# Summing the first two gate-and-up products in PSUM, and one form of the down projection for all tokens

## The chip, the cores and the metric

The kernel runs on one core of a Trainium2 chip. The core has five engines that each work through their own queue in program order and meet through semaphores: TensorE (PE in the profile; its weight loads are shown apart as PEld), VectorE (DVE), ScalarE (ACT), GpSimd (POOL) and SyncE (SP), which issues most of the DMAs. Matmuls write to PSUM, eight banks of 2 KB per partition; VectorE and ScalarE read and write PSUM and SBUF.

The metric is the device time of one execution in microseconds, the median of several. Lower is better.

## The reference

The input `x` has 2048 tokens of 448 features. The first half is an FNet mixing layer: with `n = layernorm(x)`, `h = x + Cr (n Hr) - Ci (n Hi)`, where `Cr`, `Ci` are the 2048x2048 cosine and sine matrices over the tokens and `Hr`, `Hi` those over the features. The second half is a gated feed-forward layer:

```
g = layernorm(h) @ w_gate          # 448 -> 1792
u = layernorm(h) @ w_up            # 448 -> 1792
out = h + (gelu(g) * u) @ w_down   # 1792 -> 448
```

All inputs and the output are float32.

## The kernel before

**Precision.** Every float32 operand is split in two float16 numbers, a high part (ScalarE copies the float32 tile to float16, `hi_part`, line 107) and a low part (VectorE subtracts the high part, `lo_part`, lines 111 and 113). One product is then three float16 matmuls: high x high, high x low, low x high.

**Seven products.** Large products are done in Strassen form: a 2x2 block product with seven instead of eight block products, with sums of blocks as operands and sums of results afterwards. `STRASSEN` (line 155) lists the operands for the down projection.

**Stages.** Up to about 346 us the kernel does the mixing layer and prepares the feed-forward weights, which it splits and stores to DRAM. Then comes the feed-forward layer, in 56 steps, `t = 0` to 55. The tokens are in four blocks of 512 (`q = t // 14`); in a block the 14 steps go over the tiles of 128 hidden features (`f`). A step is one `GateUp` object: the Strassen form of a pair of gate and up over one hidden tile, two token halves of 256. It has seven products into three PSUM tiles of 128x256, X, Y and Z, each of five or six matmuls (`product`, matmul at line 1015), 39 in all:

- `open`: X = A11 B11, Y = S2 T2. ScalarE copies X to SBUF as `u1` (line 1053), VectorE makes `u2 = Y + u1` (line 1025).
- `z_open`: Z = S1 T1.
- `xy`: X += A12 B21 and Y += S3 T3. ScalarE makes `g1 = gelu(X)` (line 1066), VectorE makes `u3 = Y + u1` and the hidden value `Z + u3`.
- `yz`: Y += A22 T4 and Z += S4 B22. VectorE makes the other hidden value `Y + u1`, GpSimd multiplies it by `g1` (line 1082).
- `c12_plus`: VectorE makes `c12 = Z + u2`; `c_last`: ScalarE takes its Gelu (line 1089) and GpSimd multiplies it into the first hidden value (line 1091).

From step 14 on, each step also does one unit `d = t - 14` of the down projection: 21 matmuls (`dn_mm`, line 963) on 128 tokens of each of the four quarter tiles `(hidden half, token half)`, summed over seven units into seven half banks `a0` to `a3`. Before that, `dn_sums` (GpSimd lines 1108 and 1109, VectorE line 1110) makes the five operand sums of the unit and `dn_split` its high and low parts. After seven units a `Drain` adds the seven sums to `h` (ScalarE copies two banks, VectorE adds from the banks, GpSimd adds the copies) and the result is stored.

**Other work.** The down weights are loaded, summed and split by `down_prep` in steps 0 to 13. The operands of blocks 2 and 3 are prepared in steps 14 to 40 by entries of the table `side`: an entry `(t, k)` is emitted at the k-th call `do(t, k)` of step t. The entries of `ffn_norm_act` (VectorE line 229, ScalarE line 231) stand at `k = 1` of steps 14, 20, 28 and 34; a drain begins at `k = 2` of steps 20, 27, 34, 41 and 48. At step 5 ScalarE takes a square root for the last layer normalisation and then returns to the Gelu table.

**The last block before.** For `q = 3` the hidden values go to `hq` and are split whole into `last["h"]`; the down weights are loaded a second time and the two missing weight blocks are split into `last["w"]`. After the last step, tokens with `j = 1` of the block are done in the plain form by `last_mm` (line 1178), two passes of 84 matmuls of 128x224. Meanwhile `last_sums` and `last_split` make the Strassen operands of the tokens with `j = 0`, which `last_pair_mm` (line 1220) then does in 147 matmuls, the last three units ordered by product so that their sums can be drained and stored one after the other (line 1434).

**Order.** The schedule is written by hand: each engine does its instructions in the order in which the program emits them. In a main step before, that is

```
cur.z_open(); prev.c_last(); do(t, 0); dn_split(d + 1)
dn_mm(d, range(0, 8)); cur.xy(); dn_ahead(t)
dn_mm(d, range(8, 18)); do(t, 1); do(t, 4)
cur.yz(); cur.c12_plus(); dn_mm(d, range(18, 21))
do(t, 5); do(t, 2); do(t, 3); cur = GateUp(t + 1); cur.open()
```

Of the kernel before, what the change touches and what calls it, by code (L numbers as in the profile page):

```python
# [8 lines left out]
F16 = mybir.dt.float16  # L9
# [23 lines left out]
def kernel(  # L33
# [922 lines left out]
    def strassen_mm(acc, a_of, b_of, first, last, products):  # L956

        for n in products:
            k, m = divmod(n, 3)
            a, b = STRASSEN[k]  # L960
            la, lb = ((0, 0), (0, 1), (1, 0))[m]

            PE.matmul(  # L963
                acc[k // 2][:, k % 2 * HD : (k % 2 + 1) * HD],
                a_of(la, a),
                b_of(lb, b),
                start=first and m == 0 and k % 2 == 0,
                stop=last and m == 2,
                skip_group_check=True,
            )  # L970


# [11 lines left out]
    def down_prep(t):  # L984

        n, odd = divmod(t, 2)
        if odd:
# [6 lines left out]
        elif n < NC:  # L994
            down_hi(n, 0)
            down_lo(n, 0)
            down_hi(n, 1)
# [32 lines left out]
    hh, hq = {}, {}  # L1030

    class GateUp:


        def __init__(self, t):
            self.t, self.name = t, f"{t}"
            self.q, self.f = divmod(t, NF)

            self.own = self.q > 0 or self.f % 2 == 0

        def bank(self, k):
            pool, tag = (ps_gu, "XYZ"[k]) if self.own else (ps_dn, f"a{k}")
            return pool.tile([P, 512], F32, tag=tag, name=f"p{'XYZ'[k]}_{self.name}")[:, :TQ]
# [4 lines left out]
        def open(self):  # L1048
# [4 lines left out]
            A.activation(self.u1, self.X, AF.Copy, scale=SC)  # L1053
            self.u2 = ftile("u2", 2, f"u2_{self.name}")
            plus(self.u2, self.Y, self.u1)

        def z_open(self):
            self.Z = self.bank(2)
            self.mul(self.Z, "S1", "T1", True)

        def xy(self):
            mul = [lambda: self.mul(self.X, "A12", "B21", False), lambda: self.mul(self.Y, "S3", "T3", False)]
            for m in mul if self.q == 0 else mul[::-1]:
                m()
            self.g1 = ftile("g1", 1, f"g1_{self.name}")
            A.activation(self.g1, self.X, AF.Gelu_apprx_tanh, scale=1.0 / (X_SC * W_SC))  # L1066
            u3 = ftile("u3", 1, f"u3_{self.name}")
            plus(u3, self.Y, self.u1)
            plus(self.hidden(1), self.Z, u3)

        def hidden(self, g):
            if self.q == 3:
                return hq[self.t][:, g, :]
            k, n = divmod(self.f, NF // 2)
            return hh[self.q][:, n, 2 * k + g, :]

        def yz(self):
            self.mul(self.Y, "A22", "T4", False)
            self.mul(self.Z, "S4", "B22", False)
            c21 = self.hidden(0)  # L1080
            plus(c21, self.Y, self.u1)
            G.tensor_mul(c21, c21, self.g1)  # L1082

        def c12_plus(self):
            self.c12 = ftile("c12", 1, f"c12_{self.name}")
            plus(self.c12, self.Z, self.u2)
# [6 lines left out]
    def gw_load(t):  # L1093
        gw[t] = w_tile(f"gw{t}")
        nc.sync.dma_start(gw[t], w_dram[t % NF])
# [8 lines left out]

    def dn_sums(d):
        t = dn_hid(d)
        s = dn_s[d] = late.tile([P, 5, P], F32, tag="dn_s", bufs=2, name=f"dn_s{d}")
# [3 lines left out]

    def dn_split(d):
        w = dn_w[d] = late.tile([P, 2, 7, P], F16, tag="dn_w", bufs=3, name=f"dn_w{d}")
        for src, dst in ((dn_hid(d)[:, 0:4:3], slice(0, 2)), (dn_s.pop(d), slice(2, 7))):
            hi_part(w[:, 0, dst], src)
            lo_part(w[:, 1, dst], src, w[:, 0, dst])

    outr = out.rearrange("(k g j p) d -> k j p g d", k=2, g=2, j=4)

    def dn_mm(d, products=range(21)):  # L1120
        p, n = divmod(d, NC)
        if n == 0 and 0 in products:
            acc_d[p] = [ps_dn.tile([P, 512], F32, tag=f"a{k}", name=f"acc_d{p}_{k}") for k in range(4)]
        w = dn_w[d]
        strassen_mm(
            acc_d[p],
            lambda l, a: w[:, l, a, :],
            lambda l, b: wd[n][:, l, b, :],
            n == 0,
            n == NC - 1,  # L1130
            products,
        )
# [13 lines left out]

    last = {}

    def last_begin():
        last["h"] = fpool.tile([P, 2, NF, 2 * TQ], F16, tag="hh", bufs=2, name="h_last")  # L1150
        w = ring.tile([P, N_OPS, 2 * P], F16, tag="ops", bufs=2, name="w_last")
        w = w.rearrange("p o d -> p (o d)")[:, : 4 * NC * HD]
        last["w"] = w.rearrange("p (l n k d) -> p l n k d", l=2, n=NC, k=2)

    def last_hi(t):
        hi_part(last["h"][:, 0, t % NF], hq[t].rearrange("p g t -> p (g t)"))

    def last_lo(t):
        h = last["h"][:, :, t % NF]
        lo_part(h[:, 1], hq.pop(t).rearrange("p g t -> p (g t)"), h[:, 0])  # L1160

    def last_w_hi(n):
# [335 lines left out]
```

## Time and profile before

| | |
|---|---|
| Median of 3 runs | 713.66 us (713.15 to 714.07) |
| Span of the profiled execution | 711.7 us |
| TensorE busy | 706.9 us, 5517 matmuls |
| VectorE busy | 572.3 us |
| ScalarE busy | 323.5 us |
| GpSimd busy | 235.6 us |
| Granted TensorE clock | 1.00 in all stages |

The profiled execution's time is given as its span, from the first to the last instruction; the runs are timed around it. In the profile, "idle before, releaser" is the time an engine stood still before an instruction and what ended that wait. Matmuls overlap their successors, so a group of six shown as 0.82 us takes 0.66 us of TensorE's time; the chain of work shows the latter. Lines such as L1025 or L107 are helpers that many callers share; the names of the tiles tell them apart.

### The profile page before, as it was taken

To read this page: it belongs to the slowest core of one execution; us is meant where nothing else is said; L and a number is where in the kernel's file an instruction comes from. 1 tells how busy PE (TensorE), PEld (TensorE's weight loads), DVE (VectorE), ACT (ScalarE), POOL (GpSimd) and SP (SyncE) were. 2 spreads that over 40 slices of the span, in tenths; PEclk is the share of its full clock that TensorE was granted. 3 is DMA by queue.
4 is the path that set the end of the run, shared out by engine and by line. 5 is a ranking of instruction groups with operands and counts; after the bars stand their busy time and mean duration, and the time that the engine had idled before them with its cause. 6 is when DMAs were issued, how large, how long until landed. Compare 5 with 4: busy or idle time off the path is not lost.

```text
span 711.7 us, 14303 instructions
## 1 busy us (share of the span) xinstructions
PE 706.9 (99%) x5517; PEld 536.4 (75%) x5517; DVE 572.3 (80%) x1194; ACT 323.5 (45%) x612; POOL 235.6 (33%) x277
## 2 busy tenths in 40 slices
PE   9999999999999999999999999999999999999998
PEld 6555555555555555797978899999999999999998
DVE  7997648596958979998767788787787877989787
ACT  5776424263617554543335444442444434354331
POOL 0000000000000000000365866576686766858441
PEclk9999999999999999999999999999999999999999
DMA  8798548999999989553698425648448576555401
GB/s 271 249 251 261 118 179 224 292 321 258 291 331 282 313 285 272 207 142 108 163 381 310 157 79 167 189 162 203 177 136 248 182 209 211 191 215 208 156 28 53
DMA packets 102613, 150.92 MB, mean 212 GB/s; under 512 B 61072, under 2 KB 72464, under 8 KB 102544
## 3 DMA queue, kind: packets, MB, share of 16 engines
q1 hardware_dynamic: 102400, 149.09, 68.0%
q10 hardware_dynamic: 144, 0.92, 0.4%
q8 instruction: 43, 0.70, 0.4%
q14 instruction: 26, 0.21, 0.1%
HBM read 115.90 MB, written 20.19 MB: 191 GB/s over the span
## 4 chain that ended last, share of the span: by engine, by line
PE 99%; DVE 0%; ACT 0%; POOL 0%; issue 0%; ACTq 0%; POOLq 0%
PE acc L626 33%; PE pY L1015 15%; PE acc_d L963 12%; PE pX L1015 9%; PE pZ L1015 9%; PE y L691 9%; PE acc_f L498 7%; PE last_a L1220 2%; PE last_X L1178 1%; PE last_tr L1178 1%; PE pw L101 1%; PE last_Y L1220 0%; DVE e L526 0%; ACT zs L107 0%; DVE hr L1434 0%
## 5 line engine op out<-in xcount | busy, mean ns | idle before, releaser
L626 PE MATMUL acc<-xs,ws 128*128 128x448 f16 x1248 | 237.9, 352 | 0.0
L626 PEld LDWEIGHTS <-ws 128*128 128x128 f16 x1248 | 122.1, 98 | 113.8
L1015 PEld LDWEIGHTS <-gw 128*128 128x128 f16 x1755 | 171.4, 98 | 17.2
L209 POOL TENSOR_TENSOR wd_s<-wd 128x448 f32<-128x448 f32 x7 | 8.0, 1140 | 351.0 <-DVE r_h L141 342.5
L1015 PE MATMUL pY<-hops,gw 128*128 128x256 f16 x765 | 105.3, 273 | 0.0
L963 PE MATMUL acc_d<-wd,dn_w 128*128 128x224 f16 x882 | 105.1, 259 | 0.0
L963 PEld LDWEIGHTS <-dn_w 128*128 128x128 f16 x882 | 85.0, 98 | 2.9
L113 DVE SCALAR_TENSOR_TENSOR ws<-wr,ws 128x1024 f16<-128x1024 f32 (+2 forms) x66 | 75.1, 1140 | 7.0 <-ACT ws L107 5.3
L107 ACT ACTIVATE ws<-wr 128x1024 f16<-128x1024 f32 (+2 forms) x66 | 64.4, 981 | 28.2 <-DMA wr<-in_w_seq_dram 26.7
L1025 DVE SCALAR_TENSOR_TENSOR u<-pY,u 128x256 f32<-128x256 f32 x112 | 47.0, 419 | 30.5 <-ACT c L1089 18.9
L1015 PE MATMUL pX<-hops,gw 128*128 128x256 f16 x495 | 68.7, 273 | 0.0
L1015 PE MATMUL pZ<-hops,gw 128*128 128x256 f16 x495 | 68.4, 273 | 0.0
L691 PE MATMUL y<-wh,z 128*128 128x448 f16 x336 | 66.2, 352 | 0.0
L1066 ACT ACTIVATE g<-pX 128x256 f32<-128x256 f32 x56 | 21.4, 383 | 81.3 <-PE pX L1015 74.2
L1053 ACT ACTIVATE u<-pX 128x256 f32<-128x256 f32 x56 | 21.5, 383 | 80.9 <-PE pX L1015 80.8
L691 PEld LDWEIGHTS <-z 128*128 128x128 f16 x336 | 32.9, 98 | 29.6
L111 DVE TENSOR_TENSOR dn_w<-dn_s,dn_w 128x640 f16<-128x640 f32 x42 | 52.8, 1258 | 1.1 <-ACT dn_w L107 0.8
L1082 POOL TENSOR_TENSOR hh<-hh,g 128x256 f32<-128x256 f32 x42 | 31.1, 739 | 55.8 <-DVE hh L1025 53.3
L498 PEld LDWEIGHTS <-ws 128*128 128x128 f16 x504 | 48.3, 98 | 0.9
L1091 POOL TENSOR_TENSOR hh<-hh,c 128x256 f32<-128x256 f32 x42 | 38.2, 910 | 17.9 <-ACT c L1089 17.9
L1108 POOL TENSOR_TENSOR dn_s<-hh 128x256 f32<-128x256 f32 x42 | 43.6, 1039 | 0.0
L1109 POOL TENSOR_TENSOR dn_s<-hh 128x256 f32<-128x256 f32 x42 | 43.3, 1030 | 0.0
(144 smaller groups left out, 1020.4 us busy)
## 6 DMA issues: line engine op xcount, KB each, us to landing
gw<-w_dram SPq DMA_DIRECT2D x45, 896.0 KB, 5.2
wr<-in_w_seq_dram SPq DMA_DIRECT2D x100, 256.0 KB, 4.9
w_dram<-gu_w SPq DMA_DIRECT2D x14, 896.0 KB, 6.3
gu_raw<-in_w_gu_dram SPq DMA_DIRECT2D x28, 384.0 KB, 5.9
wr<-in_w_seq_dram SPq DMA_DIRECT2D x14, 512.0 KB, 5.5
wd<-in_w_down_dram SPq DMA_DIRECT2D x14, 448.0 KB, 4.0
gw_first<-w_dram SPq DMA_DIRECT2D x7, 896.0 KB, 5.2
x<-in_x_dram SPq DMA_DIRECT2D x16, 224.0 KB, 3.8
```

The source lines that it names most:

```text
L107: A.activation(dst, src, AF.Copy, scale=scale)
L111: V.tensor_sub(dst, src, hi)
L113: V.scalar_tensor_tensor(dst, src, scale, hi, op0=ALU.mult, op1=ALU.subtract)
L498: PE.matmul(fast_sum(n, k), fast_a(n, i, lw, a), fast_b(j, lx, b), start=j == 0 and m == 0 and k % 2 == 0, stop=j == NT // 2 - 1 and m == ...
L626: PE.matmul(acc[key][:, :D], w[:, lw, block * P : (block + 1) * P], xs[c][:, lx, :], start=c == 0 and m == 0, stop=c == NT - 1 and m == 2,)
L691: PE.matmul(y[:, :D], z[p][:, lz, k, g * P : (g + 1) * P], wh[:, lw, k, :], start=k == 0 and m == 0, stop=k == 6 and m == 2,)
L963: PE.matmul(acc[k // 2][:, k % 2 * HD : (k % 2 + 1) * HD], a_of(la, a), b_of(lb, b), start=first and m == 0 and k % 2 == 0, stop=last and ...
L1015: PE.matmul(ps, w[:, wl, wa + ws, :], ops[:, m + ms, :], start=first and n == 0, stop=last and n == len(terms) - 1, skip_group_check=True,)
L1025: V.scalar_tensor_tensor(dst, ps, SC, other, op0=ALU.mult, op1=ALU.add)
L1091: G.tensor_mul(c22, c22, self.c12)
L1108: G.tensor_add(s[:, 0:2], t[:, 0:2], t[:, 2:4])
L1109: G.tensor_sub(s[:, 2:4], t[:, 1:4:2], t[:, 0:4:2])
```

## The change

**Gate and up.** The seven products and their 39 matmuls stay, in the order `x1, y1, x2, z1, y2, z2, y3`. After X = A11 B11 ScalarE copies X into the PSUM tile Y, and S2 T2 is added onto that copy by TensorE (no `u1`). ScalarE reads Y as `u2`, then S3 T3 is added to the same Y; ScalarE reads Z = S1 T1 as `m5`, and VectorE makes the second hidden value from Y and `m5`. Then A22 T4 is added to Y, and VectorE multiplies it by `g1` in one operation (no GpSimd multiplication there). `c12` is Z plus `u2` as before. From block 1 on, Y of odd steps lies in the bank `tr`.

**Order.** In the first block, parts of `down_prep` of the next step stand before `y2` and after the copy. In a main step all side work stands at the end.

**The last block.** Its hidden tiles go to `hh` like the others, in the order f = 0, 7, 1, 8, ... (`f_of`), so units of it are complete during the block. Eight units (`EARLY`) are summed and split in steps 44 to 55 into buffers that are free by then; the other six follow in the tail. All of its tokens are done with seven products by `dn_mm`, 14 units of 21 matmuls; units 42 to 48 sum into X, Y, Z and `tr`, units 49 to 55 into `a0` to `a3` and X. All `last_` functions and the second load of the down weights are gone.

```
 class GateUp:
...
+        def x1(self):
             self.X, self.Y = self.bank(0), self.bank(1)
             self.mul(self.X, "A11", "B11", True)
-            self.mul(self.Y, "S2", "T2", True)
-            self.u1 = ftile("u1", 2, f"u1_{self.name}")
-            A.activation(self.u1, self.X, AF.Copy, scale=SC)
+            A.activation(self.Y, self.X, AF.Copy)
+
+        def y1(self):
+            self.mul(self.Y, "S2", "T2", False)
             self.u2 = ftile("u2", 2, f"u2_{self.name}")
-            plus(self.u2, self.Y, self.u1)
+            A.activation(self.u2, self.Y, AF.Copy, scale=SC)
+
+        def x2(self):
+            self.mul(self.X, "A12", "B21", False)
+            self.g1 = ftile("g1", 2, f"g1_{self.name}")
+            A.activation(self.g1, self.X, AF.Gelu_apprx_tanh, scale=1.0 / (X_SC * W_SC))
...
+        def z1(self):
             self.Z = self.bank(2)
             self.mul(self.Z, "S1", "T1", True)
+            self.m5 = ftile("m5", 1, f"m5_{self.name}")
+            A.activation(self.m5, self.Z, AF.Copy, scale=SC)
+
+        def y2(self):
+            self.mul(self.Y, "S3", "T3", False)
+            plus(self.hidden(1), self.Y, self.m5)
+
+        def z2(self):
+            self.mul(self.Z, "S4", "B22", False)
+            self.c12 = ftile("c12", 2, f"c12_{self.name}")
+            plus(self.c12, self.Z, self.u2)
+
+        def y3(self):
+            self.mul(self.Y, "A22", "T4", False)
+            V.scalar_tensor_tensor(self.hidden(0), self.Y, SC, self.g1, op0=ALU.mult, op1=ALU.mult)
...
+    EARLY = [42, 43, 49, 44, 45, 50, 46, 47]
+    EARLY_AT = dict(zip((44, 46, 47, 48, 50, 51, 52, 54), EARLY))
...
     for t in range(N_GU):
...
+        if t > 0 and t != 6:
+            prev.c_last()
         if t == NF:
             dn_split(1)
...
+        cur.y1()
+        if t == 6:
+            gelu_table()
         if q == 0:
+            if t != 6:
+                cur.x2()
+            if t > 0:
+                cur.z1()
+            if t == 6:
+                prev.c_last()
+                cur.x2()
             dn_ahead(t)
...
+            down_prep(t + 1, 0)
+            cur.y2()
...
+            prev = cur
+            cur = GateUp(t + 1)
+            cur.x1()
+            down_prep(t + 1, 1)
+            prev.z2()
+            prev.y3()
...
+            if t == 5:
+
+                sd_last = root(moments[NB - 1, 1], "h_last")
...
             continue
         do(t, 0)
...
+        cur.x2()
+        cur.z1()
+        dn_mm(d, range(0, 3))
+        splits = [n for n in (d + 1, EARLY_AT.get(t - 1)) if n is not None and 1 < n and (n < 6 * NC or n != d + 1)]
+        for n in splits:
+            dn_hi(n)
+        cur.y2()
         prev = cur
         if t + 1 < N_GU:
             cur = GateUp(t + 1)
-            cur.open()
+            cur.x1()
+        prev.z2()
+        dn_mm(d, range(3, 7))
+        prev.y3()
+        for n in splits:
+            dn_lo(n)
+        dn_mm(d, range(7, 21))
+        dn_ahead(t)
+        if t in EARLY_AT:
+            dn_sums(EARLY_AT[t])
+        for k in (1, 4, 5, 2, 3):
+            do(t, k)
     prev.c_last()
...
+    late_d = [d for d in range(6 * NC, 8 * NC) if d not in EARLY]
     drain = dn_drain(5)
     drain.copy()
+    dn_sums(late_d[0])
     drain.banks01()
     drain.bank2()
     drain.bank3()
...
+    for i, d in enumerate(range(6 * NC, 7 * NC + 4)):
+        dn_mm(d)
+        if i < len(late_d):
+            dn_hi(late_d[i])
+            if i + 1 < len(late_d):
+                dn_sums(late_d[i + 1])
+            dn_lo(late_d[i])
+        if i == 2:
+            drain.sums(range(4))
+            dn_store(5)
+        if d == 7 * NC - 1:
+            drain = dn_drain(6)
+            drain.copy()
+            drain.bank2()
+            drain.bank3()
+            drain.sums(range(8))
+            dn_store(6)
```

`dn_hi(d)` and `dn_lo(d)` are the two halves of the old `dn_split`; `down_prep(t, 0)` and `down_prep(t, 1)` emit the first part and the last high part of the old `down_prep(t)`.

More of the change, by code (lines that the diff above doesn't have):

```diff
@@ L993, in down_prep @@
                 down_sums(n + 1)
[L994 to L997, printed above, removed]
+        elif not odd and n < NC:
+            if part != 1:
+                down_hi(n, 0)
+                down_lo(n, 0)
+            if part != 0:
+                down_hi(n, 1)
     SC = H_SC / (X_SC * W_SC)
```

278 lines of the change are left out of this document (78 added, 200 removed).

## The prediction

> **What bounds the kernel now.** First the page's own head and its busy times, then TensorE's waits, then the chain of work that ended last.
>
> ```profile
> span 711.7 us, 14303 instructions
> PE 706.9 (99%) x5517; PEld 536.4 (75%) x5517; DVE 572.3 (80%) x1194; ACT 323.5 (45%) x612; POOL 235.6 (33%) x277
> ```
>
> TensorE is busy 706.9 of 711.7 us. The list of what TensorE waited for has one entry after its first matmul of the program:
>
> ```profile
> PE pX L1015 <- ACT u L1053: 0.4, 1, 0.4
> ```
>
> So the time is the number of matmuls times their pace, and whatever TensorE is made to wait is added whole. The pace is read from the chain (start, length, what):
>
> ```profile
> 655.36 0.77 PE acc_d L963 x8
> ...
> 659.67 0.66 PE pX L1015 x6
> ...
> 661.63 0.77 PE acc_d L963 x8
> ...
> 663.05 0.55 PE pX L1015 x5
> ...
> 678.48 8.05 PE last_tr L1178 x84
> 686.53 8.05 PE last_X L1178 x84
> ```
>
> Six products 128x256 take 0.655 us (109 ns each), five 0.55, a 128x224 takes 8.05 / 84 = 95.8 ns. One step of the main loop is 661.63 - 655.36 = 6.27 us: 39 x 0.109 + 21 x 0.0958. Nothing is lost in it. The profiled span is 711.7; the median run, 713.66, lies 1.96 above it, which I carry along unchanged.
>
> **Tail, the gain.** The two passes last_tr and last_X (168 matmuls, for tokens with j = 1) become seven down steps of 21 matmuls, 147. The other 147 stay. 21 x 95.8 ns = **-2.0 us**. Also gone are the second load of the down weights (7 DMAs), its splits and the splits of `hq`; these were beside a full TensorE and give nothing.
>
> **The edit to gate and up.** The 39 products per step stay. Per step VectorE loses two of five PSUM adds, GpSimd one of two multiplications, ScalarE goes from three operations of 128x256 to five, which its 55% idle time takes in. What matters is the order. Y is now copied from X by ScalarE, added to by y1, read by ScalarE (u2), added to by y2, read by VectorE (into the hidden tile), added to by y3, read again. Every "read" must end before TensorE adds more. Before, X was reused only once and only behind many products. So I follow the queues, which run in program order, and count the cover in products.
>
> In a main step, with y1 starting at 0: y1 to 0.66, x2 1.20, z1 1.86, three down products 2.14, y2 2.80, x1 of the next step 3.45, z2 4.00, four down 4.38, y3 4.93, fourteen down 6.27. An unhindered reader fits: u2 would run at 0.85 to 1.23 and is needed at 2.14, the copy at 3.65 to 4.03 and is needed at 6.27. Where another ScalarE or VectorE job stands ahead of a reader, it may not. I find four such places.
>
> **Place 1, step 0.** The timeline (start, length, engine, line, out<-in):
>
> ```profile
> 346.28 0.82 PE L1015 MATMUL pX<-hops,gu_w 128*128 128x256 f16 x6
> ...
> 347.32 1.17 ACT L107 ACTIVATE zs<-e 128x448 f16<-128x448 f32 x2 [2.10 <-DVE e L526]
> ...
> 348.40 0.37 ACT L1053 ACTIVATE u<-pX 128x256 f32<-128x256 f32 x1
> 348.66 0.57 ACT L107 ACTIVATE wd<-wd 128x448 f16<-128x448 f32 x1
> 348.82 0.70 PE L1015 MATMUL pX<-hops,gu_w 128*128 128x256 f16 x5 [0.36 <-ACT u L1053]
> ...
> 349.13 1.13 ACT L107 ACTIVATE wd<-wd_s 128x1120 f16<-128x1120 f32 x1
> ...
> 349.54 0.82 PE L1015 MATMUL pY<-hops,gu_w 128*128 128x256 f16 x6
> ...
> 350.16 0.37 ACT L1066 ACTIVATE g<-pX 128x256 f32<-128x256 f32 x1
> ```
>
> ScalarE is held by `zs` until 348.40, so the copy into Y ends at 348.77 where u1 ended, and TensorE goes on at 348.82 as before, but with 12 products behind it instead of 18: +0.66. Then u2 of step 0 stands behind the two `wd` splits, in the place of `g`: 350.16 to 350.54. y1 and x2 are done at 350.02, so y2 waits 0.57 to 350.59. Before, the same stretch lost 0.17 (349.54 against 348.82 + 0.55). Sum +1.06. No ScalarE write to PSUM is in the trace; I price it as the read of 128x256 into SBUF, 0.37. Its bounds are 0 (nothing at all) and 0.57 (the longer 448 row), and only here is it uncovered, so 0.4 less or 0.2 more.
>
> **Place 2, odd steps of the first stage (t = 1, 3, 5, 7, 9, 11).** There are no down products there, so cover is thin: y1 to 0.66, x2 1.20, z1 1.86, y2 2.51, x1 3.17, z2 3.71, y3 4.26.
>
> ```profile
> 357.31 0.62 DVE L113 SCALAR_TENSOR_TENSOR wd<-wd,wd 128x448 f16<-128x448 f32 x1
> ...
> 357.86 0.42 DVE L1025 SCALAR_TENSOR_TENSOR hh<-pY,u 128x256 f32<-128x256 f32 x1
> ...
> 375.17 0.82 PE L1015 MATMUL pX<-hops,gw_first 128*128 128x256 f16 x6
> ...
> 376.02 0.38 ACT L1053 ACTIVATE u<-pX 128x256 f32<-128x256 f32 x1 [0.87 <-PE pX L1015]
> ```
>
> A reader starts 0.85 after the first of six products (376.02 - 375.17), that is 0.195 after the last is issued. m5 reads Z at 2.05; the `wd` half behind it starts 0.26 later (348.66 - 348.40) and ends at 2.88; VectorE's low part follows and takes 0.55 of its queue (357.86 - 357.31); only then comes the read of Y, 0.42, which stands behind it in the program. 2.92 + 0.55 + 0.42 + 0.05 = 3.94, where y3 is ready at 3.71: a wait of 0.25 in each, **1.5 us** for six. Even steps have only VectorE's part, with its input long there: none. Ends for one: 0 if GpSimd's and ScalarE's share is quicker than rowed, 0.7 if GpSimd slows the low part in the ratio of the two 640 rows under place 4.
>
> **Place 3, step 6.** The square root and the return to the Gelu table:
>
> ```profile
> 380.38 0.37 ACT L1053 ACTIVATE u<-pX 128x256 f32<-128x256 f32 x1
> 380.77 1.28 ACT L128 ACT_TABLE_LOAD   x1
> ...
> 382.06 0.30 ACT L128 ACTIVATE sd_h_last<-mv_h,eps_t 128x2 f32<-128x2 f32 x1
> ...
> 382.36 1.28 ACT L133 ACT_TABLE_LOAD   x1
> ...
> 383.66 0.20 ACT L133 ACTIVATE warm<-eps_t 128x1 f32<-128x1 f32 x1
> ```
>
> Counting from y1 of step 5: copy at 3.36, the 128x1120 half from 3.62 to 4.75, load and root to 6.34, u2 of step 6 to 6.72. TensorE, after the 0.25 of place 2, wants y2 at 6.36: wait 0.41. The second load and `warm` then end at 8.2, m5 at 8.58; z2 is wanted at 8.08: wait 0.55. Together **0.95**.
>
> The Trainium skill, page "ScalarE: Activation LUTs", section "What ACT_TABLE_LOAD costs", says that each switch costs a drain of about 1380 ns beside the 1283 ns of the load. By that rule, an estimate from that page: the two switches would hold ScalarE 2.76 us longer and the kernel would end near 721.9. The trace disagrees: the load follows the operation before it within 0.02 us (380.38 + 0.37, 380.77), and the next one follows the load within 0.02.
>
> What the first stage lost before goes away, since its readers change. The chain's row of one of its two hidden products, and the start of X of step 14:
>
> ```profile
> 361.27 3.97 PE y L691 x21
> ```
>
> ```profile
> 413.88 0.82 PE L1015 MATMUL pX<-hops,gw 128*128 128x256 f16 x6
> ```
>
> From 346.28 the work up to there is 536 products of 0.1092 and 42 of 128x448 (2 x 3.97), 66.5; 67.6 passed, so 1.1 was lost, 0.74 of it in place 1. The other 0.4 is credited. First stage: 1.06 + 1.5 + 0.95 - 0.4 = **+3.1**.
>
> **Place 4, steps 20, 28 and 34, where the next block is normalised.** The rows of step 34 before, and two lengths of the low part with GpSimd quiet and busy:
>
> ```profile
> 416.90 0.62 DVE L111 TENSOR_TENSOR dn_w<-hh,dn_w 128x256 f16<-128x256 f32 x1
> ...
> 417.44 0.81 DVE L111 TENSOR_TENSOR dn_w<-dn_s,dn_w 128x640 f16<-128x640 f32 x1
> ```
>
> ```profile
> 542.92 1.35 DVE L111 TENSOR_TENSOR dn_w<-dn_s,dn_w 128x640 f16<-128x640 f32 x1
> ...
> 544.64 0.42 DVE L1025 SCALAR_TENSOR_TENSOR hh<-pZ,u 128x256 f32<-128x256 f32 x1
> ...
> 544.98 0.28 DVE L1110 TENSOR_TENSOR dn_s<-hh 128x128 f32<-128x128 f32 x1
> ...
> 545.18 0.15 DVE L229 SCALAR_TENSOR_TENSOR mv_h<-mv_h,r_h_last 128x2 f32<-128x2 f32 x1
> ...
> 545.37 1.41 ACT L231 ACTIVATE xn_h<-hx,mv_h,r_h_last 128x448 f32<-128x448 f32 x2 [0.42 <-DVE mv_h L229]
> ...
> 546.68 0.95 ACT L922 ACTIVATE v<-acc_d 128x448 f32<-128x448 f32 x2
> ...
> 547.53 0.38 ACT L1053 ACTIVATE u<-pX 128x256 f32<-128x256 f32 x1
> ```
>
> ScalarE's two `xn` wait for VectorE's small `mv` operation. Before, it ran in the middle of the step, 0.54 after a read of Z (544.64, 545.18); after the change all side work stands at the end of the step, and VectorE reaches it behind the last read of Y (y3 is readable at 5.12), both low parts and the sum: 5.12 + 0.34 + 0.54 + 0.73 + 0.20 = 6.93. `xn` starts at 7.12 (+0.19), the drain's two `v` copies in steps 20 and 34 at 8.43 (+1.31), the last Gelu at 9.28 (+0.85), u2 of the next step at 9.54, ending 9.92. y2 is wanted at 6.27 + 2.14 = 8.41 and gets 9.97: wait 1.56, twice. Step 28 has no `v`: 0.72. Sum **+3.8**. Step 14 has no split and just fits. In these steps GpSimd is idle at that moment, since its multiplication waits for the same Gelu, so I take the 0.81 row; with 1.35 the three waits grow by 1.6 in all.
>
> **Smaller: step 49 and the tail.** The early splits give VectorE two low parts in eight of the last steps. My count leaves step 49, behind a drain, 0.2 short. In the tail GpSimd must make the sums of six units and drain one block:
>
> ```profile
> 681.33 2.71 POOL L954 TENSOR_TENSOR hr<-hr,v 128x224 f32<-128x224 f32 x4 [1.17 <-ACT v L922]
> 681.46 2.79 DVE L926 SCALAR_TENSOR_TENSOR hr<-acc_d,hr 128x224 f32<-128x224 f32 x8
> ...
> 415.33 0.72 POOL L1109 TENSOR_TENSOR dn_s<-hh 128x256 f32<-128x256 f32 x1
> ```
>
> Twelve sums of 0.72 and 2.71 make 11.4 us at best; with the slots of `dn_s`, two deep, I come to 14.5 to 16 us after the first tail product. The copy of bank X for the seventh product stands behind the last of these splits on ScalarE and is wanted at 8 x 2.01 - 0.29 = 15.8: a wait of 0 to 1.5, near the lower end since these ops overlap, 0.3. Together +0.5. The weights of the next step and the transposes are wanted somewhat earlier than before; I find them in time and price them at nothing, and what one came late would be added whole.
>
> **Sum.** -2.0 + 3.1 + 3.8 + 0.5 = +5.4: span 717.1, time 713.66 + 5.4 = **719.1 us**.
>
> **Rivals.**
> - *The product count decides.* VectorE and GpSimd have less to do, the readers end within their cover at every place, and only the 21 matmuls and the 0.4 are seen: 713.66 - 2.4 = 711.3, faster. For it: TensorE waited only 0.4 before. Against: place 4 needs 1.56 us less on one chain. It decides if all new waits stay under 2.4.
> - *Only the first stage stalls.* VectorE reaches `mv` by about 5.4 in steps 20, 28, 34, and place 4 is covered: 719.1 - 3.8 = 715.3. For it: it stood in mid-step before. Against: the order of the queue.
> - *GpSimd in VectorE's way.* The low parts of place 4 at 1.35 (+1.6) and, from the same slowness, the bank wait at 1.5 (+1.2): 721.9. For it: the 1.35 row, in a main step like these. Against: what GpSimd does then waits for ScalarE.
> - *A table switch costs more than its load.* Should ScalarE stand idle at each switch of step 6 for as long again as the load (2 x 1.28), u2, m5 and so y2 and z2 come that much later: 719.1 + 2.6 = 721.7. Against: the rows of place 3, where the next operation follows within 0.02.
>
> **How the numbers follow.** Chances: forecast 0.68, first stage only 0.15, product count 0.10, GpSimd in the way 0.05, the table switch 0.02. Low end 714.2, below the second rival by the 1.1 that place 1 could lack; high end 722.0 at the third and fourth. About 0.2% (1.4 us) is what a measurement of this kernel can tell from no change. Faster by more: 0.10, the product count; within: 0.05, the lower flank of the second rival; slower: 0.85.
>
> **What would show it.** Right: TensorE's wait list names ScalarE's u2 (for y2) near steps 21, 29, 35 with 0.7 to 1.6 us each, VectorE's read of Y six times at about 0.25 in the first stage, one wait for the copy into Y at step 0; the main steps otherwise keep 6.27; the tail has 294 matmuls of 95.8 ns. Wrong: no wait at steps 21, 29, 35, or waits in every step.

## The result and the profile after

The changed kernel takes 723.2 us (median of four runs, 722.64 to 724.91), the kernel before 713.41 beside it: a ratio of 1.014, 95% interval 1.0126 to 1.0155. It is slower by 9.8 us; the prediction was 719.1 with an upper end of 722.0. The profiled execution has a span of 721.3 us against 711.7. The busy times on the page of after:

```profile
PE 706.4 (98%) x5496; PEld 533.4 (74%) x5496; DVE 518.2 (72%) x1063; ACT 366.3 (51%) x726; POOL 190.8 (26%) x250
```

TensorE has the 21 matmuls less (5496 for 5517), VectorE 54 us less, GpSimd 45 us less, and ScalarE 43 us more. TensorE's busy time went down 0.5 and the span up 9.6, so the loss is waiting. TensorE's list of waits of after (what waited, for what; us in total, times, longest), which had one entry of 0.4 before (the first matmul of the program is left out in both):

```profile
PE acc_d L1171 <- ACT v L922: 3.3, 3, 2.2
PE pY L1000 <- ACT u L1048: 2.2, 4, 0.7
PE pX L1000 <- DMA gw<-w_dram: 2.1, 1, 2.1
...
PE pZ L1000 <- DVE e L526: 0.5, 1, 0.5
PE pY L1000 <- DVE hh L1010: 0.4, 1, 0.4
PE pY L1000 <- ACT pY L1043: 0.4, 1, 0.4
...
PE pZ L1000 <- ACT m L1059: 0.3, 1, 0.3
```

The list holds large single waits alone. Small ones are found by setting the starts of TensorE's products against their work, as the prediction did. Done so for the whole span, after loses in four places. The rows below are of the timeline of after, where nothing else is said.

**First stage.** X of step 0 starts at 345.96, and the second sum of Y in step 14 at 421.24, which is 4.9 us behind the work between them; before, up to the start of X of step 14, it was 1.1. Step 0, where u2 stands behind two splits on ScalarE:

```profile
348.08 0.37 ACT L1043 ACTIVATE pY<-pX 128x256 f32<-128x256 f32 x1
...
348.38 0.37 ACT L1059 ACTIVATE m<-pZ 128x256 f32<-128x256 f32 x1
...
348.64 0.56 ACT L107 ACTIVATE wd<-wd 128x448 f16<-128x448 f32 x1
349.11 1.12 ACT L107 ACTIVATE wd<-wd_s 128x1120 f16<-128x1120 f32 x1
...
350.13 0.37 ACT L1048 ACTIVATE u<-pY 128x256 f32<-128x256 f32 x1
...
350.56 0.81 PE L1000 MATMUL pY<-hops,gu_w 128*128 128x256 f16 x6 [0.70 <-ACT u L1048]
```

An odd step (t = 1), where the read of Y stands behind the low part on VectorE, and the low part behind its split on ScalarE:

```profile
355.35 0.57 ACT L107 ACTIVATE wd<-wd 128x448 f16<-128x448 f32 x1
...
355.95 0.62 DVE L113 SCALAR_TENSOR_TENSOR wd<-wd,wd 128x448 f16<-128x448 f32 x1 [2.30 <-ACT wd L107]
...
356.49 0.41 DVE L1010 SCALAR_TENSOR_TENSOR hh<-pY,m 128x256 f32<-128x256 f32 x1
...
356.96 0.49 PE L1000 MATMUL pY<-hops,gu_w 128*128 128x256 f16 x3
```

The product at 356.96 could have started at 356.12 + 0.55 = 356.67 (Z's five products before it start at 356.12): 0.29 lost. The same is lost in four more odd steps and 0.61 in step 7, where the low part took 0.94; step 0 lost 2.1 in all, step 6 another 0.8.

**The end of steps 20, 28 and 34.** Step 20: VectorE's small operation, ScalarE's two `xn`, the drain copies, then u2 of the next step:

```profile
463.45 0.15 DVE L229 SCALAR_TENSOR_TENSOR mv_h<-mv_h,r_h 128x2 f32<-128x2 f32 x1
...
463.64 1.41 ACT L231 ACTIVATE xn_h<-hx,mv_h,r_h 128x448 f32<-128x448 f32 x2 [2.91 <-DVE mv_h L229]
...
464.96 0.95 ACT L922 ACTIVATE v<-acc_d 128x448 f32<-128x448 f32 x2
465.53 0.45 PE L1171 MATMUL acc_d<-wd,dn_w 128*128 128x224 f16 x3 [0.53 <-ACT v L922]
...
466.11 0.37 ACT L1048 ACTIVATE u<-pY 128x256 f32<-128x256 f32 x1
...
466.54 0.71 PE L1000 MATMUL pY<-hops,gw 128*128 128x256 f16 x5 [0.56 <-ACT u L1048]
```

ScalarE stood idle 2.91 us for a VectorE operation of 0.15. The three places cost 1.4, 0.55 and 1.4, against the work between them: 3.4 us.

**The last weights of gate and up.** From VectorE to GpSimd to the queue SP to TensorE:

```profile
666.63 1.34 DVE L111 TENSOR_TENSOR dn_w<-dn_s,dn_w 128x640 f16<-128x640 f32 x1
...
669.19 0.85 POOL L1125 TENSOR_TENSOR dn_s<-hh 128x256 f32<-128x256 f32 x1 [1.90 <-DVE dn_w L111]
...
670.68 1.29 POOL L954 TENSOR_TENSOR hr<-hr,v 128x224 f32<-128x224 f32 x2
...
672.00 0.39 SPq L1189 DMA_DIRECT2D out_dram<-hr  x1
672.48 0.58 SPq L1085 DMA_DIRECT2D gw<-w_dram  x1
...
678.38 0.83 PE L1000 MATMUL pX<-hops,gw 128*128 128x256 f16 x6 [2.15 <-DMA gw<-w_dram]
```

The early sums have one slot, so GpSimd waits 1.90 us for VectorE's low parts to free it; its drain sums of block 4 end at 672.0; the store of that block, ahead of the load on SP, goes only then, and the load lands 5.9 us after its issue. Before, the store stood ahead of the same load too, but the drain sums ended 10 us ahead of the product that wanted the weights, where after they end 4.1 ahead of the time at which it was wanted (678.38 - 2.3). The rows of before:

```profile
660.12 1.73 POOL L954 TENSOR_TENSOR hr<-hr,v 128x224 f32<-128x224 f32 x2
...
661.88 0.39 SPq L1143 DMA_DIRECT2D out_dram<-hr  x1
...
662.36 0.42 SPq L1095 DMA_DIRECT2D gw<-w_dram  x1
...
672.04 0.82 PE L1015 MATMUL pX<-hops,gw 128*128 128x256 f16 x6
```

**The tail.** The copy of bank X for the seventh product:

```profile
697.53 3.91 POOL L954 TENSOR_TENSOR hr<-hr,v 128x224 f32<-128x224 f32 x4
...
703.69 0.72 POOL L1126 TENSOR_TENSOR dn_s<-hh 128x256 f32<-128x256 f32 x1
...
703.08 0.74 ACT L107 ACTIVATE dn_w<-dn_s 128x640 f16<-128x640 f32 x1 [4.43 <-POOL dn_s L1126]
...
704.44 0.74 ACT L107 ACTIVATE dn_w<-dn_s 128x640 f16<-128x640 f32 x1 [0.32 <-POOL dn_s L1126]
705.09 0.96 ACT L922 ACTIVATE v<-acc_d 128x448 f32<-128x448 f32 x2
...
705.66 1.50 PE L1171 MATMUL acc_d<-wd,dn_w 128*128 128x224 f16 x14 [2.21 <-ACT v L922]
```

The copy stands behind ScalarE's last split; that split waits for GpSimd's last sums, and these stand behind 3.91 us of drain sums. (The idle of 4.43 us is that of the split before the last; the last one waited 0.32.) The sum of the places, against before: -2.0 + 3.8 + 3.4 + 2.3 + 2.4 = +9.9 (4.9 - 1.1 in the first stage; the last two are the waits of 2.15 and 2.21 with the start of the matmul behind them). Taken from the start of X of step 0 to the end of the span, so without the stages ahead of it, after has 721.3 - 345.96 = 375.3 and before 711.7 - 346.28 = 365.4: +9.9.

### The profile page after: what moved, and what is told of

Same layout as the page of the kernel before. It is cut to its first block, busy times and chain, and to the rows that moved or that the text cites. A ratio compares the mean times of both kernels' runs of the same rounds, so it can differ in the third digit from the quotient of the medians.

```text
span 721.3 us, 14165 instructions
## 1 busy us (share of the span) xinstructions
PE 706.4 (98%) x5496; PEld 533.4 (74%) x5496; DVE 518.2 (72%) x1063; ACT 366.3 (51%) x726; POOL 190.8 (26%) x250
## 4 chain that ended last, share of the span: by engine, by line
PE 90%; DVE 3%; ACT 3%; POOL 2%; DMA 1%; issue 1%; ACTq 0%; SPq 0%; DVEq 0%; POOLq 0%
PE acc L626 33%; PE pY L1000 13%; PE acc_d L1171 12%; PE y L691 9%; PE pZ L1000 8%; PE pX L1000 8%; PE acc_f L498 7%; DVE dn_w L111 2%; DMA gw<-w_dram 1%; ACT wd L107 1%; POOL hr L954 1%; ACT xn_h L231 1%; DVE wd L113 0%; POOL dn_s L1125 0%; POOL dn_s L1126 0%
## 5 line engine op out<-in xcount | busy, mean ns | idle before, releaser
L1171 PE MATMUL acc_d<-wd,dn_w 128*128 128x224 f16 x1176 | 133.4, 259 | 3.3 <-ACT v L922 3.3
L1171 PEld LDWEIGHTS <-dn_w 128*128 128x128 f16 x1176 | 113.2, 98 | 6.6 <-issue 3.8
L1081 POOL TENSOR_TENSOR hh<-hh,c 128x256 f32<-128x256 f32 x56 | 45.5, 812 | 115.5 <-ACT c L1079 115.5
L1048 ACT ACTIVATE u<-pY 128x256 f32<-128x256 f32 x56 | 21.4, 382 | 79.7 <-PE pY L1000 79.6
L1125 POOL TENSOR_TENSOR dn_s<-hh 128x256 f32<-128x256 f32 x56 | 44.1, 788 | 48.9 <-DVE dn_w L111 48.8
L1010 DVE SCALAR_TENSOR_TENSOR hh<-pY,m 128x256 f32<-128x256 f32 x56 | 23.6, 421 | 43.7 <-PE pY L1000 41.3
L1010 DVE SCALAR_TENSOR_TENSOR c<-pZ,u 128x256 f32<-128x256 f32 x56 | 23.8, 424 | 37.3 <-PE pZ L1000 34.8
L1126 POOL TENSOR_TENSOR dn_s<-hh 128x256 f32<-128x256 f32 x56 | 48.8, 871 | 0.0
L107 ACT ACTIVATE dn_w<-dn_s 128x640 f16<-128x640 f32 x56 | 40.8, 729 | 13.5 <-POOL dn_s L1126 7.9
```

The lines of the kernel that those rows point to most:

```text
L107: A.activation(dst, src, AF.Copy, scale=scale)
L1010: V.scalar_tensor_tensor(dst, ps, SC, other, op0=ALU.mult, op1=ALU.add)
L1081: G.tensor_mul(c22, c22, self.c12)
L1125: G.tensor_add(s[:, 0:2], t[:, 0:2], t[:, 2:4])
L1126: G.tensor_sub(s[:, 2:4], t[:, 1:4:2], t[:, 0:4:2])
L1171: PE.matmul(ps, w[:, la, a, :], wd[n][:, lb, b, :], start=n == 0 and m == 0 and opens, stop=n == NC - 1 and m == 2, skip_group_check=True,)
```

## The experiments

The diffs are against the changed kernel, unless said. Each was timed beside the kernel before, which stayed at 713.2 to 713.4. In many executions of these kernels the granted clock fell to a half for some 3.4 us (the last section); where it matters, the executions at a clock of 1.00 are given by themselves. Those of the changed kernel are 722.64, 723.14 and 723.27.

**The store behind the load.**

```diff
-        at(side, (t0 + 4, 3), lambda p=p: dn_store(p))
+        at(side, (t0 + 4 if p < 4 else N_GU - 3, 3), lambda p=p: dn_store(p))
```

> The changed kernel, with one DMA moved: the store of finished block 4 goes to the queue SP at the end of step 53 instead of step 52, behind the last load of gate and up weights. Theory: that load came late (TensorE waited 2.1 us for it) because it stood on SP behind the store, and the store waited for GpSimd's drain sums of block 4, which came late since GpSimd had waited 1.90 us for VectorE's low part to free the single slot of the early sums. Its own slot was free some 6.8 us before it was issued. Expected: no wait for the weights in the last step, 723.2 - 2.1 = 721.1 us; GpSimd's wait stays. Rival: the load is late by itself, because its slot or the DMA engines (5.85 us to land) hold it; then the wait stays at 1 us or more, 722.2 to 723.2.

722.61 us (721.13 to 723.36), ratio 1.0128 (1.0112 to 1.0143). The wait for the weights is gone from TensorE's list, all others are as they were; the execution at a clock of 1.00 took 721.13, 2.0 below the middle one of the changed kernel. In its trace the load is issued at 665.88 instead of 672.48, 6.6 us sooner. Its place behind the late store was the cause; the load itself has time enough.

**Drain sums of block 5 early.**

```diff
-        if i == 2:
+        if i == 0:
             drain.sums(range(4))
             dn_store(5)
```

> The changed kernel, with GpSimd's first four drain sums of block 5 and its store moved forward in the tail, from behind the third split to behind the first, into a stretch where GpSimd stood idle 2.78 us. Theory: TensorE's last wait of 2.2 us is for ScalarE's copy of bank X, which stands behind ScalarE's last split, which waited 4.43 us for GpSimd's sums, which stood behind these 3.91 us of drain sums. Expected: the wait falls from 2.2 to between 0 and 0.6, 721.0 to 721.6 us. Rival: VectorE's low parts (1.3 to 2.5 us for one unit) set when the two slots of the sums come free, so the sums end where they did and the wait stays above 1.5: 722.5 to 723.2.

723.27 us (722.01 to 724.51), ratio 1.0139 (1.012 to 1.0158); 722.01 and 722.06 at a clock of 1.00, 1.1 below the changed kernel's 723.14 there, while the medians do not differ. The wait fell from 2.2 to 1.3, between what the two theories gave:

```profile
PE acc_d L1171 <- ACT v L922: 2.3, 3, 1.3
```

GpSimd's drain sums were part of the cause. In the new trace VectorE sets the pace, 2.46 us from one unit to the next, and the last split is still ahead of the copy on ScalarE. In the repaired kernel below the last split therefore goes behind the copy.

**The small operation early.**

```diff
+    def ffn_bias(q, j):
+        mv, r = moments[q, j]
+        V.scalar_tensor_tensor(mv[:, :, 1], mv[:, :, 0], -1.0, r, op0=ALU.mult, op1=ALU.mult)
...
-        V.scalar_tensor_tensor(nb, mv[:, :, 0], -1.0, r, op0=ALU.mult, op1=ALU.mult)
...
+                (0, 0, lambda q=q, j=j: ffn_bias(q, j)),
                 (0, 1, lambda q=q, j=j: ffn_norm_act(q, j, hp[q, j])),
```

> The changed kernel, with the small VectorE operation on mv (0.15 us) taken from the end of steps 14, 20, 28 and 34 to their start; the two ScalarE operations that read it stay at the end. Theory (place 4 of the prediction): u2 of the steps after 20, 28 and 34 came late because ScalarE stood waiting for that operation, which was last in VectorE's queue. Expected: TensorE's three waits for u2 and two for the drain copies around them, 3.4 us together, go to 0 to 0.3: 719.8 to 720.1 us. Rival: it is the length of the ScalarE work itself (two times 1.41, the drain's 0.95, a Gelu) or GpSimd's late multiplication that makes u2 late; then two thirds of the waits stay, 2 us or more: 721.8 to 723.2.

721.17 us (719.59 to 722.06), ratio 1.0105 (1.0088 to 1.0122); 719.59 and 720.78 at a clock of 1.00. The three waits for u2 and the two for the drain copies are gone. One operation of 0.15 us in the wrong place of a queue had cost some 3 us: 2.4 and 3.6 less than 723.14 in these two executions, 3.4 in the trace.

**Low parts behind the read of Y.**

```diff
-            down_prep(t + 1, 0)
             cur.y2()
+            down_prep(t + 1, 0)
```

> The changed kernel, with the split and sums of the down weights in the first stage issued behind the second product sum of Y instead of ahead of it, so that VectorE's read of Y stands before the low part. Theory (place 2): in odd steps the read of Y is late by the low part's 0.55, and TensorE loses about 0.29 in five steps and 0.6 in step 7. Expected: 2.0 us less, 721.2 us, TensorE's waits for hh in the first stage gone; by the prediction's own size (6 times 0.25) 1.5 less, 721.7. Rival: VectorE is behind by its whole load and not by the order, and the reads of Z and of the second Y are late instead: 722.9 to 723.5.

722.92 us (721.91 to 724.13), ratio 1.0135 (1.012 to 1.015). The stretch from X of step 0 to the first down product of step 14 is 73.48 us (346.39 to 419.87) against 74.99 (345.96 to 420.95): 1.51 less. The losses in the odd steps, 2.1 together, are all gone from the trace, as the theory said; but u2 of step 6 now loses 0.58 for 0.30 and u2 of step 8, which lost nothing, 0.28, so that 0.56 is handed on. That the net comes out at the prediction's 1.5 is by chance. The one execution at a clock of 1.00 took 721.91, 1.2 below 723.14. The load of the last weights came 0.4 later in the profiled execution.

**Splits of step 0 behind x2**, on top of the edit before.

```diff
     gw_first_load(3, nc.scalar)
-    down_prep(0)
...
             if t != 6:
                 cur.x2()
+            if t == 0:
+                down_prep(0)
```

> The kernel with the low parts behind the second read of Y, and in addition the first two splits of down weights issued behind x2 of step 0 instead of ahead of y1. Theory (place 1): u2 of step 0 stands behind ScalarE's copy, the read of Z and these two splits, 0.57 and 1.13 us, and TensorE waits 0.70 us for it. Expected: that wait gone, and the stretch from the first gate and up product to the second sum of Y of step 14 falls from 73.8 us to about 73.0, the time by 0.7 to 0.8; the 0.37 for the copy itself, which stands behind work of the stage before, stays. Rival: the splits come late instead, and the next step's copy or the low parts hold TensorE as long: 73.6 or more.

722.3 us (721.22 to 722.87), ratio 1.0123 (1.0109 to 1.0137). The wait for u2 of step 0 is gone, and the stretch is 72.96: 0.52 less where 0.7 to 0.8 were expected. The theory holds, its size was a little high.

**Step 6 without the root.** The square root of one block's variance is left out (a plain scaling stands in its place), and the two table loads with it.

```diff
-        A.activation(sd, mv[:, :, 1], AF.Sqrt, scale=1.0 / X_SC**2, bias=eps_t)
+        A.activation(sd, mv[:, :, 1], AF.Identity if tag == 'h_last' else AF.Sqrt, scale=1.0 / X_SC**2, bias=eps_t)
```

> The changed kernel without the square root of the last block's variance (the operation is kept as a plain scaling, so this block is normalised wrongly), and so without the two table loads of 1.28 us in step 6. Theory (place 3): TensorE waits 0.29 for u2 and 0.48 for m5 in step 6 because of them, and goes free: 0.8 us less. Rival: a switch costs more than its load, a drain as long again on either side; then 2 us or more would be saved. Second rival: the waits come from the split of 1.13 ahead of them; then nothing.

723.62 us (722.41 to 723.98), ratio 1.014 (1.0126 to 1.0154): in the median nothing is to be seen, since three of the four executions had the clock fall; the fourth took 722.41, 0.7 below 723.14. The stretch is 73.92, so 1.07 less than with the loads. Of this 0.78 is step 6, as read from the trace, and 0.3 is step 7, whose loss fell from 0.61 to 0.30. Both together are far from the 2 us or more of a drain beside each load; and since the split of 1.13 stayed where it was, the loads were the cause in step 6.

**All repairs**, the five edits together, and the last split behind the copy of bank X:

```diff
-        if i < len(late_d):
+        if i < len(late_d) - 1:
...
             drain = dn_drain(6)
             drain.copy()
+            dn_split(late_d[-1])
```

> The changed kernel with all repairs: low parts behind the second read of Y, the splits of step 0 behind x2, the small mv operation at the start of its step, the store of block 4 behind the last load of weights, the drain sums of block 5 early in the tail, and the last split behind the copy of bank X. Theory: the waits are separate and add up: from a run of the changed kernel at full clock, 723.1, go 1.5 + 0.8 + 3.4 + 2.1 + 2.2, so 713.1, the time before within 0.2%; what is left of the gain of 2.0 is eaten by the first stage (copy 0.4, step 6 0.8, and the matmul that waits for bank Z). With no wait above 1 us the granted clock stays at 1.00 to the last matmul. Rival: the waits hide one another, and something else is late behind them: 715 us or more.

713.37 us (712.94 to 713.66, 11 runs), ratio 0.9998 (0.9989 to 1.0007): the time before, as expected (713.1). The waits add up. Its list of waits, without the first matmul of the program:

```profile
PE pZ L1003 <- DVE e L529: 0.5, 1, 0.5
PE pY L1003 <- ACT u L1051: 0.4, 1, 0.4
PE pY L1003 <- ACT pY L1046: 0.4, 1, 0.4
PE pZ L1003 <- ACT m L1062: 0.3, 1, 0.3
```

No wait is left behind step 14; the tail is one run of 308 matmuls. The gain of 2.0 is spent in the first stage, which still loses 2.9 (1.2 ahead of y1 of step 0, 1.1 in step 6, 0.3 in step 8, the rest in pieces below 0.2) where before lost 1.1.

**The tail alone.** Gate and up as before, the tail new and repaired; the diff is against the kernel before.

```diff
-        if 1 < d + 1 < 6 * NC:
-            dn_split(d + 1)
+        for n in (d + 1, EARLY_AT.get(t - 1)):
+            if n is not None and 1 < n and (n < 6 * NC or n != d + 1):
+                dn_split(n)
...
+        if t in EARLY_AT:
+            dn_sums(EARLY_AT[t])
```

> One half of the change alone: gate and up as in the kernel before (no ScalarE copy, VectorE's five additions, its order of the loop), but the last 512 tokens' down in seven products, with the early sums and splits, and with the repairs of the store, the drain sums of block 5 and the last split. Theory: the tail's 21 matmuls of 95.8 ns are the only gain in the change and cost nothing by themselves: 713.2 - 2.0 = 711.2 us. Rival: the early splits and sums need the room on VectorE and GpSimd that the edit to gate and up makes (VectorE is busy 80% before and GpSimd multiplies twice a step), so without it TensorE waits in the last eight steps: 713.2 or more.

720.77 us (720.43 to 721.52), ratio 1.0107 (1.0091 to 1.0122). My theory fell: this is 7.5 slower, not 2.0 faster. TensorE waits in seven of the last steps, 8.3 us. The entry in its list of waits, and the timeline of step 45:

```profile
PE pY L998 <- DVE u L1008: 8.3, 7, 1.5
```

```profile
610.73 0.82 DVE L111 TENSOR_TENSOR dn_w<-hh,dn_w 128x256 f16<-128x256 f32 x1
611.48 1.35 DVE L111 TENSOR_TENSOR dn_w<-dn_s,dn_w 128x640 f16<-128x640 f32 x1
612.74 0.94 DVE L111 TENSOR_TENSOR dn_w<-hh,dn_w 128x256 f16<-128x256 f32 x1
613.61 1.34 DVE L111 TENSOR_TENSOR dn_w<-dn_s,dn_w 128x640 f16<-128x640 f32 x1
614.88 0.41 DVE L1008 SCALAR_TENSOR_TENSOR u<-pY,u 128x256 f32<-128x256 f32 x1
...
615.34 0.71 PE L998 MATMUL pY<-hops,gw 128*128 128x256 f16 x5 [1.48 <-DVE u L1008]
```

Four low parts in a row hold VectorE for 4.2 us ahead of its read of Y. With the order of before, the tail with seven products needs the room on VectorE that the edit to gate and up makes. (Another order within the step was not tried.)

**Gate and up alone.** The new form with its repairs, and the tail of before (its two passes, splits and loads).

```diff
-    EARLY = [42, 43, 49, 44, 45, 50, 46, 47]
+    EARLY = []
...
+            at(side, (t + 1, 1), lambda n=n, k=k: last_w_lo(n, k))
...
+    for g in range(2):
+        last_mm(1, g, banks[g : g + 1])
```

> The other half of the change alone: gate and up in the new form with the repairs of the first stage, of the mv operation and of the store, but the down of the last 512 tokens as before (168 matmuls in the plain form, 147 in the form with seven products, its splits beside the last fourteen steps). Theory: TensorE has the 21 matmuls of 95.8 ns more and nothing else changes: 713.4 + 2.0 = 715.4 us. Rival: the splits that this tail needs in the last fourteen steps hold the readers of Y and Z, and waits come back: 716.5 or more.

714.93 us (714.75 to 715.62), ratio 1.0021 (1.0013 to 1.003), 1.6 above the kernel with all repairs. From X of step 0 to the end it is 713.4 - 346.16 = 367.24 against 711.7 - 346.53 = 365.17: 2.07, the 21 matmuls, as the theory had it. The rest is the start of that X, which moves by some tenths from execution to execution.

**Two more edits to the first stage**, on top of all repairs.

```diff
     cur = GateUp(0)
     cur.x1()
+    for g in range(2):
+        fast_halves(N_STEPS - 1, g)
+    z_turn(NP - 1)
...
-            down_prep(t + 1, 0)
+            if t != 6:
+                down_prep(t + 1, 0)
...
-            down_prep(t + 1, 1)
+            if t != 5:
+                down_prep(t + 1, 1)
+            if t == 6:
+                down_prep(6, 1)
             prev.z2()
             prev.y3()
+            if t == 6:
+                down_prep(7, 0)
```

> The changed kernel with all repairs, and two more in the first stage: ScalarE makes its copy into Y of step 0 ahead of the two splits of zs of the stage before (it waited for them, 0.37 us of TensorE's time), and the 1.13 us split of step 5 and its low part go behind the square root and the two table loads, so that u2 and m5 of step 6 come sooner (0.42 and 0.32). Theory: these waits are from ScalarE's order alone; 713.4 - 0.4 - 0.7 = 712.3 us, below the time before (713.3). Rival: what is moved back comes late itself (the last block's z for the second sum of hidden products, the down weights of step 7), and nothing is won: 713.4 or more.

712.59 us (712.12 to 713.98), ratio 0.999 (0.9981 to 0.9999): 0.8 below before, the fastest of all, if barely. The copy's wait and both of step 6 are gone, but the wait for u2 in step 8, which lost 0.28 with all repairs, now loses 1.18: ScalarE's split ahead of u2 waits there for GpSimd's sums, which were moved back with the rest:

```profile
393.67 0.81 PE L987 MATMUL pY<-hops,gw 128*128 128x256 f16 x6 [1.02 <-ACT u L1035]
```

**A wait by hand.** In the repaired kernel ScalarE's copy of the first two banks of block 6 is made four times more, and in a second kernel six times.

```diff
             drain = dn_drain(6)
-            drain.copy()
+            for _ in range(5):
+                drain.copy()
```

> The repaired kernel (713.4 us, no wait of TensorE above 0.6 after the first matmul) with one wait put in by hand: ScalarE copies the first two banks of block 6 four times more, 0.86 us each, ahead of the copy that the seventh product needs. From the slack of 1.1 us in its trace TensorE should wait about 2.4 us at one place. Theory: after an idle of about 2 us the granted clock falls to a half for some 3.5 us in part of the executions, as the traces of the changed kernel with one repair showed behind waits of 1.8 to 2.6 us, so one group of runs lies at 713.4 + 2.4 = 715.8 and another 1.7 higher, at 717.5. Rival: the dips belong to the two places where they were seen and not to the wait; then all runs lie at 715.8.

> As the run before with six copies more, a wait of about 4.1 us. Theory: the longer the wait, the surer the dip; all or nearly all executions at 713.4 + 4.1 + 1.7 = 719.2 us. Rival: the dip does not depend on the length, and part of the runs lie at 717.5.

Four copies: TensorE waited 2.27 us; one execution took 715.51, the other four 717.34 to 718.02 (ratio 1.0052, 1.0039 to 1.0066). Six copies: 4.03 us; 718.99 to 719.86 and one of 721.26, ratio 1.0089 (1.0076 to 1.0103). Near what the theory gave (715.8 and 717.5; 719.2), but for the 721.26, whose mean clock is 0.995 where the others have 0.997 or 0.998. The waits of "1.8 to 2.6" in the first of the two texts should be 2.2 to 2.6: in the two traces with a wait of 1.8 or 1.9 for the weights the fall came later, behind the 2.2 of the tail. The windows of 1 us of the execution with four copies (busy us of TensorE, its weight loads, VectorE, ScalarE, GpSimd, each with its count; then the granted clock, the share of the DMA engines and their GB/s):

```profile
697.00:698.00 1.00, 0.00 (x0) 0.00 (x0) 0.00 (x0) 1.00 (x3) 0.00 (x0) 1.00 0.00 0
698.00:699.00 1.00, 0.72 (x8) 0.70 (x8) 0.01 (x1) 1.00 (x4) 0.70 (x2) 0.95 0.00 0
699.00:700.00 1.00, 1.00 (x8) 0.83 (x6) 1.00 (x2) 0.58 (x1) 0.92 (x2) 0.50 0.00 0
700.00:701.00 1.00, 1.00 (x7) 0.82 (x6) 1.00 (x2) 0.00 (x0) 1.00 (x2) 0.50 0.00 0
701.00:702.00 1.00, 1.00 (x8) 0.80 (x6) 0.97 (x4) 0.00 (x0) 0.71 (x2) 0.50 0.00 0
702.00:703.00 1.00, 1.00 (x10) 0.93 (x9) 0.47 (x2) 0.00 (x0) 0.86 (x2) 0.84 0.00 0
703.00:704.00 1.00, 1.00 (x13) 1.00 (x12) 0.00 (x0) 0.00 (x0) 1.00 (x3) 1.00 0.00 0
```

TensorE is back at 698.3; for 0.1 + 3 + 0.3 us, 3.4 in all, the clock is 0.50. The counts take in matmuls that lie partly in a window: 7 or 8 where the clock is 0.50, 13 where it is 1.00. From start to start one takes 187 ns in the fall, for 95.8 at full clock.

## Why the prediction was wrong

Its direction and the places in gate and up were right, the sum was 4.5 short, and nearly all of that is in one paragraph, the one on step 49 and the tail.

- *Tail gain, -2.0.* Right: 5496 matmuls, and 2.07 between the kernels with the new and the old tail.
- *Places 1 to 3, +3.1.* The places and mechanisms were right; the trace gives 3.8, from 1.3 + 2.1 + 0.8 - 0.4. Place 1 was low: the read of Z into m5 also stands ahead of the splits in step 0, which I had not counted (348.38 to 348.75 in the trace), so step 0 lost 2.1 for the 1.8 that the prediction's terms amount to with before's own loss. Place 2 was low as well, 2.1 for 1.5: its own rows give 0.23 a step (3.94 - 3.71), the trace 0.29 in five steps and 0.61 in step 7, with the slow low part that it had named as its upper end. Place 3 was 0.8 for 0.95.
- *ScalarE's write to PSUM.* Taken as the read into SBUF, 0.37; the row at 348.08 shows 0.37.
- *Place 4, +3.8.* Measured 3.4 (1.4, 0.55, 1.4 for 1.56, 0.72, 1.56), and gone with one operation moved. The long low part of 1.35 did not come there: 0.82 at 462.52. The first low part held VectorE 0.33 (462.19 to 462.52) for the 0.54 that was counted, and so `mv` came some 0.2 sooner.
- *Weights of the next step, in time and priced at nothing.* This failed: 2.3. The prediction shows no working for it; what it missed is what stands ahead of the load on SP. The early sums are new work for GpSimd in the last steps, its drain sums go later, the store waits for them, and the load waits for the store. The prediction said what a late load would cost ("added whole"), and gave it no chance.
- *Tail, 0.3 of a bound of 0 to 1.5.* This failed by size: 2.4 (2.2 of it in one wait), above the bound. The mechanism was named, and counted with GpSimd's quiet lengths: 0.72 for a sum and 2.71 for the drain, where the tail's rows have up to 1.30 (at 687.91) and 3.91, and the slots of the sums held GpSimd another 2.78 and 0.76. The last split ended 17.7 us after the tail's start (705.18 - 687.47), for the 14.5 to 16 of the prediction. Choosing the lower end "since these ops overlap" was the wrong way round: VectorE's and GpSimd's work that overlapped was longer here, not shorter. Moving the drain sums alone took back 0.9 of the 2.2; the rest went with the last split behind the copy, in the kernel with all repairs.

With 2.3 more for the weights, 1.9 for the tail (step 49, priced at 0.2, shows no wait), 0.7 for the first stage and 0.4 less at place 4, the sum of 5.4 becomes the 9.9 measured. The signs that the prediction named came (u2 near steps 21, 29 and 35, the read of Y in six odd steps, one copy in step 0), but none of them tells of the two terms that failed. No rival gave the time. Of the rivals, the product count and the first stage alone are out (place 4 stalls). The slow GpSimd had the right cause, but put it in place 4 and gave the tail 1.5 at most. The table switch is out: the root follows its load, and the load the operation ahead of it, within 0.02 us (382.16 + 1.13 and 383.31; 383.31 + 1.28 and 384.60), and the whole edit to step 6 was worth 1.07.

## What to carry to other kernels

When an edit gives an engine new work late in a kernel, follow that engine to every queue behind it, the stores' among them, and look for loads that share their queue with a store: here a store that waited for GpSimd held a load of weights by 6.6 us. Count overlapping VectorE and GpSimd work with its rows from a busy stretch, and put the reads that free a PSUM bank ahead of splits and small helpers in each queue; six such reorderings took back 9.8 us without taking away an operation. A change with two halves can need both: in the orders tried, the new tail alone lost 7.5 us, new gate and up alone 1.6, and both, put in order, nothing.

## What the runs showed of the hardware

A wait of TensorE can cost more than its length. In eight of the traces the granted clock fell to 0.50 for 3.4 us, each time behind an idle of TensorE of 2.2 to 4.0 us; matmuls of 95.8 ns then took 187, and 1.7 us were lost. It comes in part of the executions: the trace of the changed kernel has waits of 2.15 and 2.21 and no fall. By the mean clock (0.998 or less) the executions with a fall were 1 of 4 of the changed kernel, 15 of 24 of the six kernels with one or two edits, 4 of 5 with a wait of 2.27 put in by hand and 4 of 4 with 4.03; with four copies they took 717.7 - 715.5 = 2.2 us more, of which the trace gives 1.7 to the fall. Where no wait behind the first matmul was above 1.5 us (the kernel before, all repairs, the two more edits, the tail alone, gate and up alone), the mean clock was 0.999 or 1.00 in all 58. What a wait between 1.5 and 2.2 does stays open: two of 1.82 and 1.87 had no fall behind them. The wait put in by hand is at a place where falls had been seen; without the wait that place had none, and another place was not tried.

The Trainium skill, page "TensorE: Matmul & The Clock Gate", section "HAM oscillation — how this bites in real kernels", warns of idle gaps above some 3.4 us; these traces show the fall behind gaps well below that, from 2.2 us on. The Trainium skill, same page, section "What's actually happening", tells of a window of about 3.4 us that runs by itself. The length of the fall here, 3.4 us, agrees with it; that the fall comes in some executions only would fit such a window too, which no run here shows.
